# Two attentions in one program: the local scores stored place-minor, the inverses cut in three, two groups of weight splits moved

## The chip, the cores and the metric

The kernel runs on one core of a Trainium2 chip. The metric is the device time of one execution in microseconds (us); three runs of the kernel before gave 1580.18, 1580.74 and 1582.28 us, a median of 1580.74 us.

## The reference

Two independent attention layers over 2048 positions, 32 heads of 18 columns each (576 in all), float32. Layer A is local: each position attends to 8 places, 0, 2, ..., 14 positions back; places before the start are masked. Layer B is full attention without a mask. The two results stand side by side in the output.

```python
# A: W, dil = 8, 2 ; idx = pos - 2 * (0..7)
logits = einsum("bhsd,bhswd->bhsw", q, k[idx]) * scale      # 8 scores per position
attn = softmax(where(idx >= 0, logits, -1e9))
a = einsum("bhsw,bhswd->bhsd", attn, v[idx]) @ wo
# B: full attention
b = einsum(softmax(einsum(q, k) * scale), v) @ wo
out = concatenate([a, b], axis=-1)
```

## The kernel before, in words

**The stages.** First TensorE makes the projections of both layers (to about 416 us). Then come 512 numbered steps, the main part: B's 8 groups of four heads (`NG`), times 4 blocks of 512 queries (`NB`), times 16 tiles of 128 keys (`NT`). The steps end with B's last output product.

**One step.** TensorE makes four scores of 128 keys by 512 queries (L388), the sums of the step before with the values (`weigh`, L898), and two to four score tiles of a later block that serve only to find each query's maximum (L239). ScalarE takes the exponentials of the scores (L398, L401). VectorE (DVE) reduces the tiles of L239 to maxima (L256, L258 and L272): three of them in a plain step. TensorE has few PSUM banks for these tiles, so that it waits when VectorE is behind. Some steps ("producing" ones) also hold products with an output weight (L1239) and take about twice as long.

**Layer A.** The 2048 positions are 8 places `j` of 256 positions (`local(j)`), each held as 128 partitions (32 heads times 4 parts) by 64 positions. Nearly all of it is on GpSimd (POOL): products of queries and shifted keys (`match`, L1042), their sums (L1045), the last sum into the score tile `lg` (L1049, 8 window scores times 64 positions; for j = 0 with masks by L1052), subtraction of the maximum (`lower`, L1065), sums of the exponentials (`total`, L1076), multiplication by the inverse (`share`, L1083), and the weighted values (`weighted`, L1090 to L1096). VectorE finds the maximum over the window in four pieces of 16 positions (`most`, L1059, tile `am`) and the inverses in two pieces of 32 (`inverses`, L1080); ScalarE takes the exponentials (`exponents`, L1069), in two halves in some places and in one piece in others. The result is split into a high and a low part (L1100, L1105) and goes through DRAM to TensorE.

**What sets the order.** Every engine runs its queue in the order in which the program is written. `plan(start, pieces)` puts a piece into the agenda of a step, and `due()` writes the pieces of a step at its end. `local(j)` starts at step 10 + 55 j (`A_FROM`, `GAP`); its pieces have fixed steps within the place: the four maxima at 30 to 33, `lower` at 33, exponentials at 34 and 35, totals at 36, inverses at 37 and 38, `share` at 38, `weighted` from 38 on, the split at 86 and 87 (60 and 61 in the last place). So a piece of GpSimd has no time of its own: GpSimd takes it when all pieces written earlier are done.

**Output weights.** Both `wo` matrices are loaded in five chunks of rows into tile `y` by the DMA queue of SyncE (`load_wo`, L1000) and split three steps later by GpSimd into a high part (a cast, L176) and a low part (a subtraction, L177), into `wohi` and `wolo` for A and into freed tiles `qs` and `ks` for B. A's chunks begin at step 28 and B's at step 404 (`STEPS * (NG - 2) + 20`), one every four steps; the fifth of B has a memset of `y` ahead (L997). The first use of A's splits is the first producing step, of B's the sums of the last group.

Of the kernel before, what the change touches and what calls it, by code (L numbers as in the profile page):

```python
# [7 lines left out]
F32 = mybir.dt.float32  # L8
# [4 lines left out]
AX = mybir.AxisListType  # L13
# [7 lines left out]
W = 8  # L21
DIL = 2
NG = H // 4
# [3 lines left out]
MASKED = -1e9 / SCALE  # L27
# [3 lines left out]
SUB = AB // 4  # L31
HALO = DIL * (W - 1)

STEPS = NB * NT
# [24 lines left out]
def ap(t, *dims):  # L59

    return bass.AP(tensor=t.tensor, offset=t.offset, ap=[list(t.ap[0])] + [list(d) for d in dims])
# [8 lines left out]
def two_attentions(ctx: ExitStack, tc, xa, wa, woa, xb, wb, wob, out):  # L70
# [5 lines left out]
    nc = tc.nc  # L76
# [109 lines left out]
    def plan(start, pieces):  # L186
        for n, f in pieces:
            agenda[start + n].append(f)
# [326 lines left out]
    with (tc.tile_pool(name="x", bufs=1, side="right") as xp,  # L515
# [117 lines left out]
        if True:  # L633

            third = D // 3
# [193 lines left out]
            for k in range(2, 14):  # L829
                n = 46 if k == 2 else 36 + 4 * k  # L830
# [33 lines left out]
            for k, b in order:  # L864
                c = turn_of[k]
                n = min(128, 3 * D - 128 * c)
# [26 lines left out]
    work = ctx.enter_context(tc.tile_pool(name="work", bufs=1, reuse_waits="tile"))  # L893
# [98 lines left out]
    def load_wo(k, src, *pieces):  # L992

        raw = work.tile([128, D], F32, name="y", bufs=4)
        n = 0
        if len(pieces) == 4:
            nc.gpsimd.memset(raw, 0.0)  # L997
            n = 128
        for at, c0, m in pieces:
            load(raw[at : at + m], src[c0 : c0 + m])  # L1000
            n = max(n, at + m)
        if k == "a":
            hi = work.tile([128, D], F32R, name="wohi", bufs=5)
            lo = work.tile([128, D], F32R, name="wolo", bufs=5)
        else:

            c = len(wo.get(k, []))
            hi, lo = (ap(t[:, 0, 0, :] if len(t.shape) == 4 else t[:, 0, :], (1, NB * 1024))[:, D * c : D * c + D]
                      for t in sets[(NG - 3) % 3])
        wo.setdefault(k, []).append((hi, lo))  # L1010
        later(3, lambda: split_on(nc.gpsimd, hi[:n], lo[:n], raw[:n]))


    def local(j):

        st = {}
# [11 lines left out]
        def window(t, c):  # L1028

            return ap(t[:, 2 * c, HALO:], (HALO + SUB, 2), (-DIL, W), (1, SUB))  # L1030

        def wide():
            return work.tile([128, 2, W, SUB], F32, name="pr", bufs=2)

        def match(c):
            if c < DH // 2:
                if c % 2 == 0 and c:
                    room = work.tile([128, DH, SUB], F32, name="aohi", bufs=1)
                    pr = ap(room, (W * SUB, 2), (SUB, W), (1, SUB))
                else:  # L1040
                    pr = wide()
                nc.gpsimd.tensor_mul(pr, ap(st["q"][:, 2 * c], (SUB, 2), (0, W), (1, SUB)), window(st["k"], c))  # L1042
                st["prs"] = st.get("prs", []) + [pr]
            if c > 1:
                nc.gpsimd.tensor_add(st["prs"][0], st["prs"][0], st["prs"][c - 1])  # L1045
            if c == DH // 2:
                st["pr"] = st["prs"][0]
                lg = st["lg"] = work.tile([128, W, SUB], F32, name="lg", bufs=1)
                nc.gpsimd.tensor_add(lg, st["pr"][:, 0], st["pr"][:, 1])  # L1049
                if j == 0:  # L1050
                    for w in range(1, W):
                        nc.gpsimd.memset(lg[:32, w, : DIL * w], MASKED)  # L1052

        def over_window(op, name, i, of):

            if i == 0:
                st[name] = work.tile([128, SUB], F32, name=name, bufs=1)
            at = slice(SUB // of * i, SUB // of * (i + 1))
            nc.vector.tensor_reduce(st[name][:, at], st["lg"][:, :, at].rearrange("p w n -> p n w"), axis=AX.X, op=op)  # L1059

        def most(i, of):
            over_window(ALU.max, "am", i, of)

        def lower():
            nc.gpsimd.tensor_sub(st["lg"], st["lg"], ap(st["am"], (0, W), (1, SUB)))  # L1065

        def exponents(i, of):
            at = slice(W // of * i, W // of * (i + 1))
# [7 lines left out]
            nc.gpsimd.tensor_add(t[:, :half], src[:, :half], src[:, half : 2 * half])  # L1076

        def inverses(n):
            half = st["as"][:, 0, SUB // 2 * n : SUB // 2 * n + SUB // 2]
            nc.vector.reciprocal(half, half)  # L1080

        def share():
            nc.gpsimd.tensor_mul(st["lg"], st["lg"], ap(st["as"], (0, W), (1, SUB)))  # L1083
# [44 lines left out]
        def sums_of_a(h):  # L1128
# [12 lines left out]
            def add():  # L1141
# [7 lines left out]
        MOST = ((30, 0, 4), (31, 1, 4), (32, 2, 4), (33, 3, 4))  # L1149
        EXPS = ((34, 0, 2), (35, 1, 2)) if A_FROM + GAP * j + 35 not in producing else ((35, 0, 1),)  # L1150
        TOTAL = ((36, 0), (36, 1), (36, 2))
        INV = ((37, 0), (38, 1))
        LOWER, SHARE, MATCH, WEIGHT = 33, 38, 5, 38
        UP, REST, PUT0, PUT1 = (60, 61, 64, 66) if j == NJ - 1 else (GAP + 31, GAP + 32, GAP + 34, GAP + 35)
        pieces = [(LOWER, lower), (SHARE, share), (UP, upper), (REST, rest), (PUT0, lambda: put(0)), (PUT1, lambda: put(1))]

        pieces[:0] = [(at, lambda f=f, args=args: f(*args)) for f, ats in ((most, MOST), (exponents, EXPS), (total, TOTAL),
                                                                          (inverses, INV)) for at, *args in ats]
        for c in range(DH // 2 + 1):
            pieces.append((MATCH + 5 * min(c, DH // 2 - 1) // 2, lambda c=c: match(c)))  # L1160
# [8 lines left out]
        for n in range(2):  # L1169
            free, begin = turns[-1] if turns else 0, start + PUT1 + 5  # L1170
            at = max(free, begin)
# [172 lines left out]
        sums[t, b, h] = (y,)  # L1344

    for k, src, start, chunks in (
        ("a", woa, 28, [[(0, 128 * c, 128)] for c in range(4)] + [[(64 * r, 512, 64) for r in range(2)]]),
        ("b", wob, STEPS * (NG - 2) + 20,
         [[(0, 126 * c, 126)] for c in range(4)] + [[(32 * i, 504 + DH * i, DH) for i in range(4)]]),
    ):  # L1350
        plan(start, [(4 * c, lambda k=k, src=src, ch=ch: load_wo(k, src, *ch)) for c, ch in enumerate(chunks)])
    for j in range(NJ):
        plan(A_FROM + GAP * j, local(j))
# [31 lines left out]
    while step < ALL:  # L1385
        n, kt = divmod(step, NT)
        g, b = divmod(n, NB)
# [10 lines left out]
        a = left // 2 if left != 1 or given[0] >= given[1] else 1  # L1398
# [73 lines left out]
```

## Time and profile before

| what | value |
|---|---|
| median of 3 runs | 1580.74 us (1580.18 to 1582.28) |
| the profiled execution's own time | 1580.53 us |
| its span from first to last instruction | 1578.7 us |
| TensorE clock granted in it | 1.000 |
| TensorE, VectorE, ScalarE, GpSimd busy | 99%, 89%, 75%, 61% of the span |
| the 512 steps | from about 416 us to the end |

The rows that the prediction quotes have, in a timeline, the start in us, the length in us, engine, line, operation, the tiles (written from read), the count, and in brackets how long the engine was idle before and who released it. Neighbouring equal instructions are merged into one row. An instruction of VectorE starts before the one ahead has ended, so that from start to start it takes less than its length. In a table of groups the columns are count, busy time in us, mean length in ns, and the idle time before.

### The profile page before, as it was taken

The page shows a single profiled execution, that of the slowest core. Times are in us where ns is not written, and L with a number is a line of the kernel's source. Part 1 is how long each engine was busy: PE and PEld are TensorE (multiplying, and loading weights), DVE is VectorE, ACT ScalarE, POOL GpSimd, SP SyncE. Part 2 cuts the span into 40 slices and gives each one's busy share as a digit, 9 for nine tenths or more (in the row PEclk, how much of TensorE's full clock was granted, in tenths as well). Part 3 has the DMA queues.
Part 4 walks back from the last instruction along what each step waited for, and adds up shares of the span by engine and source line. Part 5 has one row for each costly group of instructions (what it writes and reads, how often), then busy time and mean ns, then how long its engine had stood idle before and what let it go on. Part 6 is the DMA issues. An engine that isn't in the chain of part 4 may idle for free.

```text
span 1578.7 us, 34691 instructions
## 1 busy us (share of the span) xinstructions
PE 1570.7 (99%) x13400; PEld 950.1 (60%) x13400; DVE 1397.6 (89%) x2381; ACT 1183.5 (75%) x1918; POOL 966.0 (61%) x820
## 2 busy tenths in 40 slices
PE   9999999999999999999999999999999999999998
PEld 7999998888544444445444445444444454555776
DVE  5299999999999999999999999999999999999433
ACT  7323441211699999999999999999999999898444
POOL 2305852201257997994996995995995997930100
PEclk9999999999999999999999999999999999999999
DMA  9848954523321253253235316423523142234211
GB/s 263 220 131 208 261 183 126 162 75 100 75 56 55 64 115 90 70 141 100 60 88 145 81 47 155 104 61 103 136 58 98 37 109 71 78 118 157 86 39 61
DMA packets 190149, 173.12 MB, mean 110 GB/s; under 512 B 123120, under 2 KB 136944, under 8 KB 188256
## 3 DMA queue, kind: packets, MB, share of 16 engines
q1 hardware_dynamic: 185120, 159.36, 36.3%
q0 software_dynamic: 4032, 10.63, 3.1%
q8 instruction: 105, 1.72, 0.5%
q10 hardware_dynamic: 832, 0.92, 0.2%
q14 instruction: 60, 0.49, 0.1%
HBM read 97.47 MB, written 72.95 MB: 108 GB/s over the span
## 4 chain that ended last, share of the span: by engine, by line
PE 96%; POOL 2%; DMA 1%; DVE 1%; issue 1%; ACT 0%; SPq 0%; POOLq 0%; ACTq 0%; DVEq 0%
PE po L898 31%; PE bank L239 19%; PE bank L498 16%; PE bank L388 10%; PE bank L1239 8%; PE pair L388 7%; PE bank L424 4%; POOL pr L1045 1%; POOL aohi L1042 0%; DMA first<-xb 0%; DMA raw<-wa 0%; DVE mx L256 0%; POOL ks L177 0%; POOL ohi L844 0%; DMA da<-ohi 0%
## 5 line engine op out<-in xcount | busy, mean ns | idle before, releaser
L239 PE MATMUL bank<-ks,qs 54*128 54x256 f32 (+1 forms) x2526 | 755.1, 372 | 1.3 <-DVE mx L256 0.6
L256 DVE TENSOR_REDUCE mx<-bank 128x1 f32<-128x512 f32 x1024 | 679.9, 684 | 59.5 <-PE bank L239 33.5
L239 PEld LDWEIGHTS bank<-ks,qs 54*128 54x128 f32 x2526 | 414.1, 184 | 428.4 <-DVE mx L272 312.5
L398 ACT ACTIVATE e<-bank 128x512 f32<-128x512 f32 x1024 | 611.2, 603 | 72.9 <-PE bank L388 66.0
L898 PE MATMUL po<-ee,v 128*19 128x512 f32 x2048 | 536.7, 599 | 0.0
L898 PE MATMUL po<-e,v 128*19 128x512 f32 x2048 | 531.4, 599 | 0.0
L401 ACT ACTIVATE ee<-pair 128x1024 f32<-128x1024 f32 x478 | 487.7, 1020 | 1.1 <-PE pair L388 0.4
L388 PE MATMUL bank<-qs,ks 56*128 56x512 f32 x1092 | 460.8, 441 | 0.0
L258 DVE TENSOR_REDUCE mx<-bank 128x2 f32<-128x512 f32 x546 | 355.8, 684 | 20.2 <-PE bank L239 7.2
L272 DVE TENSOR_REDUCE mx<-bank 128x2 f32<-128x512 f32 x478 | 326.1, 682 | 0.0
L388 PE MATMUL pair<-qs,ks 56*128 56x512 f32 x956 | 248.3, 396 | 0.0
L388 PEld LDWEIGHTS bank<-qs,ks 56*128 56x128 f32 x1092 | 194.4, 183 | 15.6 <-ACT e L398 7.1
L1090 POOL TENSOR_TENSOR pr<-lg,akv 128x1024 f32<-128x1024 f32 x72 | 157.2, 2205 | 0.6
L840 ACT ACTIVATE ohi<-bank 128x512 f32<-128x512 f32 (+1 forms) x56 | 30.6, 595 | 147.5 <-issue 125.5
L388 PEld LDWEIGHTS pair<-qs,ks 56*128 56x128 f32 x956 | 137.8, 185 | 0.0
L898 PEld LDWEIGHTS po<-ee,v 128*19 128x19 f32 x2048 | 69.6, 96 | 109.6 <-issue 109.6
L498 PE MATMUL bank<-xhi,ahi 64*128 64x512 f32 x448 | 116.1, 390 | 0.1
L498 PE MATMUL bank<-xlo,ahi 64*128 64x512 f32 (+1 forms) x448 | 104.1, 392 | 0.2 <-POOL xlo L546 0.2
L498 PE MATMUL bank<-xhi,alo 64*128 64x512 f32 x416 | 102.3, 390 | 0.0
L1042 POOL TENSOR_TENSOR pr<-aq,akv 128x1024 f32<-128x1024 f32 x40 | 87.7, 2199 | 17.0 <-PE bank L239 15.9
L1092 POOL TENSOR_TENSOR pr<-pr 128x512 f32<-128x512 f32 x72 | 91.3, 1293 | 0.6
L546 POOL TENSOR_TENSOR alo<-raw,ahi 128x512 fp32r<-128x512 f32 x13 | 16.8, 1294 | 113.1 <-ACT ahi L545 111.8
(210 smaller groups left out, 2369.5 us busy)
## 6 DMA issues: line engine op xcount, KB each, us to landing
do<-n SPq DMA_DIRECT2D x28, 512.0 KB
da<-ohi SPq DMA_DIRECT2D x52, 256.0 KB
akv<-da SPq DMA_DIRECT2D x64, 175.5 KB
out<-y SPq DMA_DIRECT2D x32, 288.0 KB
qs<-dqk SPq DMA_DIRECT2D x30, 288.0 KB
ks<-dqk SPq DMA_DIRECT2D x30, 288.0 KB
at<-dao SPq DMA_DIRECT2D x64, 128.0 KB
rec<-drec SPq DMA_DIRECT2D x29, 256.0 KB
```

The lines of the kernel that those rows point to most:

```text
L239: return nc.tensor.matmul(ps, qs[rows_, b, p, 128 * t : 128 * t + 128], ks[rows_, p, 512 * k + at : 512 * k + at + n], start=True, stop=True)
L256: nc.vector.tensor_reduce(mx[:, r, p, t, k : k + 1], ps, axis=AX.X, op=ALU.max)
L258: nc.vector.tensor_reduce(mx[:, r, p, t, 2 * k - 2 : 2 * k], ps.rearrange("q (h n) -> q h n", h=2), axis=AX.X, op=ALU.max)
L272: nc.vector.tensor_reduce(mx[:, :, p, t, 2 * k - 2 + i], ps.rearrange("q (h n) -> q h n", h=2), axis=AX.X, op=ALU.max)
L388: nc.tensor.matmul(ps, ks[at, p, 128 * kt : 128 * kt + 128], qs[at, b, p], start=True, stop=True)
L398: nc.scalar.activation(e, ps, AF.Exp, scale=SCALE)
L401: nc.scalar.activation(whole, both_scores[0], AF.Exp, scale=SCALE)
L498: nc.tensor.matmul(ps, a, b, start=start, stop=stop)
L898: nc.tensor.matmul(po[32 * i : 32 * i + 19], vs[g][:, kt, 19 * i : 19 * i + 19], es[i], start=kt == 0, stop=kt == NT - 1)
L1090: nc.gpsimd.tensor_mul(at, ap(st["lg"], (0, 2), (SUB, W), (1, SUB)), window(st["v"], n))
L1092: nc.gpsimd.tensor_add(at[:, :, :4], at[:, :, :4], at[:, :, 4:])
L1239: nc.tensor.matmul(sums_[r], a, b, start=i == 0, stop=i == len(both[r]) - 1)
```

## The change

GpSimd's last sum of a place goes into a new tile `lgt` (`by` in the code) in which the 8 window scores of a position stand side by side (64 positions times 8), written with a stride of 32 bytes; the masks of place 0 go there too. `most` reads this tile, so that the 8 values of a maximum are neighbours and not 256 bytes apart. `lower` reads it with a stride of 32 bytes and writes `lg` in the old layout; what follows is as before. The inverses are three pieces of 22, 21 and 21 positions at 37, 38 and 39, and `share` and all of `weighted` move by one step, from 38 to 39. The chunks of A's output weight begin at step 2 (before: 28), those of B's at step 459 (before: 404).

```diff
-                lg = st["lg"] = work.tile([128, W, SUB], F32, name="lg", bufs=1)
-                nc.gpsimd.tensor_add(lg, st["pr"][:, 0], st["pr"][:, 1])
+                st["lg"] = work.tile([128, W, SUB], F32, name="lg", bufs=1)
+                by = st["by"] = work.tile([128, SUB, W], F32, name="lgt", bufs=1)
+                nc.gpsimd.tensor_add(by.rearrange("p n w -> p w n"), st["pr"][:, 0], st["pr"][:, 1])
                 if j == 0:
                     for w in range(1, W):
-                        nc.gpsimd.memset(lg[:32, w, : DIL * w], MASKED)
+                        nc.gpsimd.memset(by[:32, : DIL * w, w], MASKED)
...
-            nc.vector.tensor_reduce(st[name][:, at], st["lg"][:, :, at].rearrange("p w n -> p n w"), axis=AX.X, op=op)
+            nc.vector.tensor_reduce(st[name][:, at], st["by"][:, at], axis=AX.X, op=op)
...
         def lower():
-            nc.gpsimd.tensor_sub(st["lg"], st["lg"], ap(st["am"], (0, W), (1, SUB)))
+            nc.gpsimd.tensor_sub(st["lg"], st["by"].rearrange("p n w -> p w n"), ap(st["am"], (0, W), (1, SUB)))
...
         def inverses(n):
-            half = st["as"][:, 0, SUB // 2 * n : SUB // 2 * n + SUB // 2]
-            nc.vector.reciprocal(half, half)
+            third = st["as"][:, 0, (0, 22, 43)[n] : (22, 43, SUB)[n]]
+            nc.vector.reciprocal(third, third)
...
-        INV = ((37, 0), (38, 1))
-        LOWER, SHARE, MATCH, WEIGHT = 33, 38, 5, 38
+        INV = ((37, 0), (38, 1), (39, 2))
+        LOWER, SHARE, MATCH, WEIGHT = 33, 39, 5, 39
...
-        ("a", woa, 28, [[(0, 128 * c, 128)] for c in range(4)] + [[(64 * r, 512, 64) for r in range(2)]]),
-        ("b", wob, STEPS * (NG - 2) + 20,
+        ("a", woa, 2, [[(0, 128 * c, 128)] for c in range(4)] + [[(64 * r, 512, 64) for r in range(2)]]),
+        ("b", wob, STEPS * (NG - 1) + 11,
```

On GpSimd's queue at the end of the matches of the last place, j = 7, these rows stood before (`y`, `qs` and `ks` are B's output weight and its two parts; `o`, `n` and `rec` belong to B's blocks; the rest is the place's own):

```order
L1042 TENSOR_TENSOR pr<-aq,akv 128x1024
L1045 TENSOR_TENSOR pr<-pr,aohi 128x1024
L936 TENSOR_TENSOR o<-o,rec 128x512
L937 CAST n<-o 128x512
L176 CAST qs_3591<-y 126x576
L177 TENSOR_TENSOR ks_3592<-y,qs_3591 126x576
L997 MEMSET y 128x576
L1042 TENSOR_TENSOR aohi<-aq,akv 128x1024
L1045 TENSOR_TENSOR pr<-pr 128x1024
L1045 TENSOR_TENSOR pr<-pr,aohi 128x1024
L1049 TENSOR_TENSOR lg<-pr 128x512
```

Now the same stretch of GpSimd's queue reads so, with the score tile as its last row:

```order
L1042 TENSOR_TENSOR pr<-aq,akv 128x1024
L1045 TENSOR_TENSOR pr<-pr,aohi 128x1024
L936 TENSOR_TENSOR o<-o,rec 128x512
L937 CAST n<-o 128x512
L1042 TENSOR_TENSOR aohi<-aq,akv 128x1024
L1045 TENSOR_TENSOR pr<-pr 128x1024
L1045 TENSOR_TENSOR pr<-pr,aohi 128x1024
L1050 TENSOR_TENSOR lgt<-pr 128x8x64
```

The split and the memset are gone from here, as are the three splits ahead of them in the same place; all five now stand behind the whole work of the place. A's five splits have gone the other way, to the front of place 0: three ahead of its first match, one behind its second, one behind its third.

On VectorE's queue in place 1 the inverses (tile `as`) stood before so, among the maxima of B (`mx`):

```order
L258 TENSOR_REDUCE mx<-bank_9232 128x2
L1080 RECIPROCAL as<-as 128x32
L258 TENSOR_REDUCE mx<-bank_9248 128x2
L272 TENSOR_REDUCE mx<-bank_9242 128x2
L258 TENSOR_REDUCE mx<-bank_9263 128x2
L1080 RECIPROCAL as<-as 128x32
L256 TENSOR_REDUCE mx<-bank_9285 128x1
L272 TENSOR_REDUCE mx<-bank_9278 128x2
L256 TENSOR_REDUCE mx<-bank_9300 128x1
L933 RECIPROCAL den<-den 128x16
L282 TENSOR_REDUCE m_82<-mx 128x16
```

Now the same stretch of VectorE's queue reads:

```order
L258 TENSOR_REDUCE mx<-bank_9235 128x2
L1081 RECIPROCAL as<-as 128x22
L258 TENSOR_REDUCE mx<-bank_9251 128x2
L272 TENSOR_REDUCE mx<-bank_9245 128x2
L258 TENSOR_REDUCE mx<-bank_9266 128x2
L1081 RECIPROCAL as<-as 128x21
L256 TENSOR_REDUCE mx<-bank_9281 128x1
L272 TENSOR_REDUCE mx<-bank_9274 128x2
L256 TENSOR_REDUCE mx<-bank_9296 128x1
L1081 RECIPROCAL as<-as 128x21
L933 RECIPROCAL den<-den 128x16
```

The third piece stands one step behind the second, and GpSimd's `share`, which needs all pieces, with it. The order of TensorE's and ScalarE's instructions is the same in both kernels.

## Prediction

> **What bounds the kernel now.** I read the page's head, its busy times and the chain of work that ended last, first.
>
> ```profile
> span 1578.7 us, 34691 instructions
> PE 1570.7 (99%) x13400; PEld 950.1 (60%) x13400; DVE 1397.6 (89%) x2381; ACT 1183.5 (75%) x1918; POOL 966.0 (61%) x820
> PE 96%; POOL 2%; DMA 1%; DVE 1%; issue 1%; ACT 0%; SPq 0%; POOLq 0%; ACTq 0%; DVEq 0%
> ```
>
> The chain is TensorE nearly throughout. None of the edits touches a TensorE instruction, so they can only shorten or lengthen steps in which TensorE is held up by another engine. I looked for such steps in VectorE's timeline, at the small maxima `am` of place 2.
>
> ```profile
> 722.13 0.68 DVE L272 TENSOR_REDUCE mx<-bank 128x2 f32<-128x512 f32 x1
> 722.73 1.49 DVE L256 TENSOR_REDUCE mx<-bank 128x1 f32<-128x512 f32 x2
> 724.14 0.68 DVE L272 TENSOR_REDUCE mx<-bank 128x2 f32<-128x512 f32 x1
> 724.74 0.68 DVE L256 TENSOR_REDUCE mx<-bank 128x1 f32<-128x512 f32 x1
> 725.34 0.37 DVE L1059 TENSOR_REDUCE am<-lg 128x16 f32<-128x128 f32 x1
> 725.62 0.68 DVE L256 TENSOR_REDUCE mx<-bank 128x1 f32<-128x512 f32 x1
> 726.22 0.68 DVE L272 TENSOR_REDUCE mx<-bank 128x2 f32<-128x512 f32 x1
> ...
> 728.30 0.68 DVE L272 TENSOR_REDUCE mx<-bank 128x2 f32<-128x512 f32 x1
> ```
>
> From L272 to L272 is one step. A plain one takes 2.01 us (722.13 to 724.14), and there VectorE has time left: three maxima of 0.60 us from start to start (724.14 to 724.74) make 1.80, so 0.21 us is spare. With an `am` the step takes 2.08 us (724.14 to 726.22, and again to 728.30): an `am` takes 0.29 us from start to start (725.34 to 725.62), 0.08 more than is spare. Here VectorE sets the step, by 0.08 us. That is the size of what this change can win in a place.
>
> **The change part by part.** The prices come from the groups of instructions.
>
> ```profile
> L256 DVE TENSOR_REDUCE mx<-bank 128x1 f32<-128x512 f32 x1024 | 679.9, 684 | 59.5 <-PE bank L239 33.5
> ...
> L1059 DVE TENSOR_REDUCE am<-lg 128x16 f32<-128x128 f32 x32 | 11.9, 373 | 0.5 <-POOL lg L1049 0.5
> ...
> L1049 POOL TENSOR_TENSOR lg<-pr 128x512 f32<-128x512 f32 x8 | 10.3, 1285 | 0.6
> ...
> L282 DVE TENSOR_REDUCE m<-mx 128x16 f32<-128x96 f32 x32 | 7.8, 243 | 0.4
> ...
> L177 POOL TENSOR_TENSOR ks<-y,qs 126x576 fp32r<-126x576 f32 (+1 forms) x5 | 7.1, 1422 | 0.4
> ...
> L933 DVE RECIPROCAL den<-den 128x16 f32<-128x16 f32 x29 | 7.0, 243 | 0.0
> ...
> L1080 DVE RECIPROCAL as<-as 128x32 f32<-128x32 f32 x16 | 5.5, 343 | 0.0
> ...
> L176 POOL CAST qs<-y 126x576 fp32r<-126x576 f32 (+1 forms) x5 | 3.3, 666 | 0.0
> ...
> L737 POOL MEMSET vs<- 128x128 f32 x4 | 1.4, 380 | 17.1 <-DMA dv<-vs 17.1
> ...
> L997 POOL MEMSET y<- 128x576 f32 x1 | 0.6, 588 | 0.0
> ...
> L314 POOL MEMSET m<- 128x32 f32 x2 | 0.2, 114 | 0.0
> ```
>
> *Term A, the small maxima.* L282 also makes 16 outputs, from 96 neighbouring values, in 243 ns; L256 takes 684 for 512. Between them lie 1.06 ns a value, so 128 neighbouring values should take 277 ns, against 373 with the wide stride: 96 ns less. From start to start that is 0.29 - 0.10 = 0.19 us, which fits into the spare 0.21. So the overrun of 0.08 us goes. The first of a place's four is partly taken up by the idle time ahead of it, so I count 26 of 32: 26 x 0.08 = 2.1 us won. The ends: nothing (the stride is not what makes it slow) and 32 x 0.08 = 2.6 us.
>
> [...]
>
> *Term B, the inverses.* L1080 and L933 differ by 16 values and 100 ns, 6.25 ns each, so pieces of 22 and 21 take about 280 ns: 24 x 0.28 = 6.7 us in place of 16 x 0.343 = 5.5. A piece of 32 exceeds the spare time by little and two in succession are mostly absorbed; three shorter ones fit, but the third joins steps that have another small operation (in place 1 `den` and `m`). The ends are 16 x (0.343 - 0.28) = 1.0 us won and 6.7 - 5.5 = 1.2 us lost. I take 0.2 us won, near the middle.
>
> *Term C, B's splits leave place 7.*
>
> ```profile
> 1316.38 0.68 DVE L272 TENSOR_REDUCE mx<-bank 128x2 f32<-128x512 f32 x1
> ...
> 1318.14 0.39 DVE L1059 TENSOR_REDUCE am<-lg 128x16 f32<-128x128 f32 x1 [0.49 <-POOL lg L1049]
> ...
> 1319.05 0.68 DVE L272 TENSOR_REDUCE mx<-bank 128x2 f32<-128x512 f32 x1
> ```
>
> This is the only place where VectorE waits for GpSimd's score tile, 0.49 us, and the step takes 2.67 us (1316.38 to 1319.05), 0.66 over a plain one. Four splits and the memset leave the queue ahead of that tile: 4 x (0.67 + 1.42) + 0.59 = 8.9 us earlier, far more than is needed. Won: 0.66 us; at least 0.49. Their new place is behind the place's work, where GpSimd is free and the sums that need them are more than ten steps off. SyncE's queue is passed too: the chunk loads stand among the loads of the last group, and the latest of these, `rec`, moves back by the four short loads of the fifth chunk; what GpSimd makes of `rec` waits for TensorE afterwards anyway. Cost nothing; without that cover some 2 us.
>
> *A's splits* go where GpSimd waits now:
>
> ```profile
> 427.94 4.35 POOL L1042 TENSOR_TENSOR pr<-aq,akv 128x1024 f32<-128x1024 f32 x2 [15.87 <-PE bank L239]
> ...
> 452.16 0.21 POOL L176 CAST mt<-mt 128x32 fp32r<-128x32 f32 x1 [19.87 <-DVE mt L290]
> ```
>
> Of 36 us idle the first four splits take 8.4 and the three chunk loads ahead of the matches delay these a little; the `mt` at 452 comes no later. The fifth split takes the room of one that stood among place 0's matches before, so the tile of place 0 is ready as early as now. Nothing won, nothing lost.
>
> *Term D, `share` one step later.*
>
> ```profile
> 490.54 1.27 POOL L1049 TENSOR_TENSOR lg<-pr 128x512 f32<-128x512 f32 x1
> ...
> 496.13 0.38 DVE L1059 TENSOR_REDUCE am<-lg 128x16 f32<-128x128 f32 x1
> ...
> 513.41 1.28 POOL L1083 TENSOR_TENSOR lg<-lg,as 128x512 f32<-128x512 f32 x1 [2.58 <-DVE as L1080]
> ...
> 605.39 1.30 POOL L1049 TENSOR_TENSOR lg<-pr 128x512 f32<-128x512 f32 x1
> ...
> 607.72 0.38 DVE L1059 TENSOR_REDUCE am<-lg 128x16 f32<-128x128 f32 x1
> ```
>
> Between the third and the fourth of these rows the view by stretches of time gives the busy time of TensorE, its weight loads, VectorE, ScalarE and GpSimd, in this order:
>
> ```profile
> 513.41:606.69 93.28, 93.28 (x737) 41.09 (x740) 88.17 (x147) 92.33 (x139) 91.90 (x69) 1.00 0.40 92
> ```
>
> From place 0's `share` to the score tile of place 1 GpSimd is busy 91.90 of 93.28 us. It has nothing to catch up with: what moves `share` moves the tile. The third piece comes one step, 2.0 us, after the second and is 0.07 shorter, so `share` is 1.93 us later against the steps. The tile ended at 606.69, 1.03 us ahead of its `am`: now the `am` comes first and VectorE waits 1.93 - 1.03 = 0.9 us. Behind it stand B's maxima, and TensorE waits for those; the spare 0.2 us of the step is taken off: **0.7 us lost**, in place 1 alone. In the other places the tile is ready 4 us or more ahead, as in place 0 (491.81 against 496.13); place 7 gains by term C. The ends: nothing (GpSimd catches up after all) and 0.9.
>
> *Terms E and F, GpSimd's strides of 32 bytes.* No row shows such a sum. The nearest is the memset L737, whose values lie 76 bytes apart: 380 ns for 128, where L997 and L314 (588 for 576, 114 for 32, so 0.87 ns each) would give 198. That is 1.4 ns a value more, 0.73 us for 512 values. Or nothing, as a sum at 1285 ns takes 2.5 ns a value already and the write may hide below it. I take 0.35 us for each, the middle, since a sum moves three streams of which one changes. For the score tile (E) it adds to the wait of place 1: 0.35 us lost. For `lower` (F) ScalarE is next:
>
> ```profile
> 502.95 1.28 POOL L1065 TENSOR_TENSOR lg<-lg,am 128x512 f32<-128x512 f32 x1 [4.26 <-DVE am L1059]
> ...
> 504.37 0.43 ACT L1069 ACTIVATE lg<-lg 128x256 f32<-128x256 f32 x1
> ...
> 614.62 1.27 POOL L1065 TENSOR_TENSOR lg<-lg,am 128x512 f32<-128x512 f32 x1 [4.09 <-DVE am L1059]
> ...
> 616.04 0.43 ACT L1069 ACTIVATE lg<-lg 128x256 f32<-128x256 f32 x1
> ...
> 1207.20 1.28 POOL L1065 TENSOR_TENSOR lg<-lg,am 128x512 f32<-128x512 f32 x1 [1.83 <-DVE am L1059]
> ...
> 1208.62 0.43 ACT L1069 ACTIVATE lg<-lg 128x256 f32<-128x256 f32 x1
> ```
>
> In places 0, 1 and 6 the first exponential starts 0.14 us after `lower` ends (504.37 against 504.23); the `am` ahead is 0.10 shorter, so 0.24 us is free. Longer by 0.35, `lower` holds ScalarE, and B's exponentials behind it, 0.1 us in each of the three: 0.3 us lost. The ends for E and F together: nothing, and 0.73 + 3 x 0.49 = 2.2.
>
> [...]
>
> *The sum.* Won 2.1 + 0.2 + 0.66 = 2.96; lost 0.7 + 0.35 + 0.3 = 1.35; together 1.6 us won. The profiled execution took 1580.53 us by itself, so 1578.9; the median of the runs stands 0.2 us above it. I predict **1579.1 us**.
>
> **The rivals.** *First, GpSimd does not hold place 1 back*: strides cost nothing and the wait of term D is absorbed by idle time that the sums hide. Then 2.96 us are won, 1580.74 - 2.96 = 1577.8 us, and with term A at its end and B's 1.0 as far as 1576.5. For it: place 1's next steps hold a copy that waits for TensorE in any case. Against it: GpSimd's 91.90 busy us of 93.28.
>
> *Second, the other side: GpSimd's strided sum is slow.* If each of the two takes L us longer, the loss is L in place 1 and L - 0.24 in three places: 0.7 + L + 3 (L - 0.24). It meets the 2.96 won at L = 0.75, just above the bound from L737. At twice the time of now, L = 1.28, it is 0.7 + 1.28 + 3.1 = 5.1, net 2.1 us lost: 1582.9 us; at L = 1.6 it is over 0.2%. For it: the one strided row takes nearly twice the time. Against it: 1285 ns leaves room to hide it. [...]
>
> *Third, `am` does not get shorter.* Then A is 0 and the sum is 0.5 us lost: 1581.2 us. L282 reads few values, too, and may not stand for it.
>
> **How the numbers follow.** I give my forecast (within 1 us of 1579.1) 0.50, the first rival 0.25, the second 0.15, the third 0.10. A measurement of this kernel tells about 0.2%, 3.2 us, from no change: below 1577.6 or above 1583.9 us. Of the first rival half, 0.13, ends below 1577.6, and I add 0.07 for a larger term A or B under my forecast: faster 0.20. Of the second, half, 0.08, ends above 1583.9, and I add 0.02 for a wait that I have not seen: slower 0.10. The rest, 0.70, is no change. The range, 1576.9 to 1581.8 us, leaves out the first rival's far end and most of the second.
>
> **What the profile after would show.** A: L1059 at about 277 ns, steps around it of 2.01 us. B: 24 inverses of about 280 ns. C: no idle time ahead of place 7's first `am`. D: VectorE idle about 0.9 to 1.3 us ahead of place 1's first `am`, released by GpSimd's tile. E, F: the tile and `lower` at 1.3 to 2.0 us, idle time of ScalarE ahead of the first exponential of places 0, 1 and 6. A row of `am` at 370 ns would take A away; a tile over 2 us would make the kernel slower.

## The result, and the profile after

The changed kernel takes **1578.18 us** (median, 1577.69 to 1578.78), the kernel before, beside it, 1580.93 us: a ratio of 0.9981 with a 95% interval of 0.9974 to 0.9989 (over all runs, so not quite that of the two medians). That is 2.75 us less; 1.6 had been forecast. The profiled executions took 1577.96 and 1580.53 us, 2.57 us apart. The head of the page after:

```profile
span 1576.2 us, 34697 instructions
PE 1568.2 (99%) x13400; PEld 947.9 (60%) x13400; DVE 1394.8 (88%) x2389; ACT 1183.3 (75%) x1918; POOL 968.8 (61%) x820
PE 92%; DMA 3%; POOL 2%; issue 1%; DVE 1%; SPq 1%; ACT 0%; POOLq 0%; ACTq 0%; DVEq 0%
```

TensorE is still the chain. The groups with the changed operations (count, busy us, mean ns, idle time before them):

```profile
L1060 DVE TENSOR_REDUCE am<-lgt 128x16 f32<-128x128 f32 x32 | 8.8, 275 | 0.7 <-POOL lgt L1050 0.7
L1081 DVE RECIPROCAL as<-as 128x21 f32<-128x21 f32 x16 | 4.4, 277 | 0.0
L1081 DVE RECIPROCAL as<-as 128x22 f32<-128x22 f32 x8 | 2.2, 279 | 0.0
...
L1066 POOL TENSOR_TENSOR lg<-lgt,am 128x512 f32<-128x512 f32 x8 | 12.5, 1560 | 45.8 <-DVE am L1060 45.8
L1050 POOL TENSOR_TENSOR lgt<-pr 128x512 f32<-128x512 f32 x8 | 10.4, 1297 | 0.6
```

An `am` takes 275 ns (before 373), the inverses 277 to 279, the tile 1297 (before 1285), `lower` 1560 (before 1281). VectorE at place 2, where a step with an `am` took 2.08 us before:

```profile
724.44 0.68 DVE L272 TENSOR_REDUCE mx<-bank 128x2 f32<-128x512 f32 x1
725.04 0.68 DVE L256 TENSOR_REDUCE mx<-bank 128x1 f32<-128x512 f32 x1
725.64 0.28 DVE L1060 TENSOR_REDUCE am<-lgt 128x16 f32<-128x128 f32 x1
725.83 0.69 DVE L256 TENSOR_REDUCE mx<-bank 128x1 f32<-128x512 f32 x1
726.44 0.68 DVE L272 TENSOR_REDUCE mx<-bank 128x2 f32<-128x512 f32 x1
```

From L272 to L272 it is 2.00 us, and the `am` takes 0.19 us from start to start (725.64 to 725.83). VectorE at the first `am` of places 1 and 7:

```profile
608.20 0.28 DVE L1060 TENSOR_REDUCE am<-lgt 128x16 f32<-128x128 f32 x1 [0.70 <-POOL lgt L1050]
...
1316.20 0.27 DVE L1060 TENSOR_REDUCE am<-lgt 128x16 f32<-128x128 f32 x1
```

The wait has left place 7 and stands in place 1, 0.70 us long.

To see where the time went, every step's length was worked out from TensorE's timeline: step k runs from the start of the k-th group of eight L898 products to the next, counted from 0 at about 416 us. Up to step 0 the executions differ by up to 1.1 us (416.3 to 417.4; 1.0 between two profiles of the changed kernel itself), so the last column starts there. By the program's numbers steps 44, 99 and 374 have the first exponential of places 0, 1 and 6, steps 95 and 96 the first two `am` of place 1 and step 425 the first of place 7; what step 80 waits for is told at e9. All in us:

| kernel | steps 44, 99, 374 | step 80 | 95 + 96 | step 425 | step 0 to the end |
|---|---|---|---|---|---|
| before | 2.03, 2.04, 2.03 | 2.17 | 4.38 | 2.67 | 1162.43 |
| after | 2.20, 2.19, 2.19 | 2.18 | 4.78 | 2.01 | 1159.84 |
| e1 layout only | 2.19, 2.20, 2.20 | 2.17 | 4.28 | 2.58 | 1160.58 |
| e2 splits only | 2.04, 2.05, 2.03 | 2.18 | 4.38 | 2.08 | 1161.37 |
| e3 inverses only | 2.02, 2.03, 2.02 | 2.66 | 4.57 | 4.54 | 1165.10 |
| e4 after, two pieces | 2.20, 2.19, 2.18 | 2.18 | 4.28 | 2.00 | 1159.41 |
| e5 `lower` in halves | 2.20, 2.18, 2.19 | 2.83 | 4.28 | 1.99 | 1159.90 |
| e6 `am` of four | 2.19, 2.18, 2.19 | 2.17 | 4.26 | 2.53 | 1160.49 |
| e7 `share` at 40 | 2.19, 2.20, 2.18 | 2.18 | 4.72 | 2.00 | 1159.52 |
| e8 strides by place | 2.19, 2.19, 2.18 | 2.59 | 4.45 | 2.01 | 1160.90 |
| e9 third inverse at 40 | 2.19, 2.19, 2.18 | 3.86 | 4.28 | 2.01 | 1164.56 |
| e10 A's splits only | 2.03, 2.05, 2.02 | 2.19 | 4.39 | 2.59 | 1162.01 |
| e11 pairs, two pieces | 2.19, 2.18, 2.18 | 2.18 | 4.28 | 2.01 | 1159.31 |
| e12 after again | 2.18, 2.19, 2.19 | 2.53 | 4.48 | 2.00 | 1159.96 |

### The profile page after: what moved, and what is told of

It reads as the page before. It is cut to its first block, busy times and chain, and to the rows that moved or that the text cites. A ratio compares the mean times of both kernels' runs of the same rounds, so it can differ in the third digit from the quotient of the medians.

```text
span 1576.2 us, 34697 instructions
## 1 busy us (share of the span) xinstructions
PE 1568.2 (99%) x13400; PEld 947.9 (60%) x13400; DVE 1394.8 (88%) x2389; ACT 1183.3 (75%) x1918; POOL 968.8 (61%) x820
## 4 chain that ended last, share of the span: by engine, by line
PE 92%; DMA 3%; POOL 2%; issue 1%; DVE 1%; SPq 1%; ACT 0%; POOLq 0%; ACTq 0%; DVEq 0%
PE po L898 30%; PE bank L239 19%; PE bank L498 15%; PE bank L388 9%; PE bank L1240 8%; PE pair L388 7%; PE bank L424 4%; DMA drec<-den 1%; DMA ks<-dqk 1%; POOL pr L1045 1%; POOL xlo L546 1%; DMA raw<-xa 0%; DMA rec<-drec 0%; DVE mx L256 0%; PE bank L664 0%
## 5 line engine op out<-in xcount | busy, mean ns | idle before, releaser
L256 DVE TENSOR_REDUCE mx<-bank 128x1 f32<-128x512 f32 x1024 | 679.5, 683 | 59.7 <-PE bank L239 33.2
L898 PE MATMUL po<-ee,v 128*19 128x512 f32 x2048 | 536.7, 599 | 0.0
L898 PE MATMUL po<-e,v 128*19 128x512 f32 x2048 | 531.4, 599 | 0.1
L401 ACT ACTIVATE ee<-pair 128x1024 f32<-128x1024 f32 x478 | 487.6, 1020 | 0.5
L272 DVE TENSOR_REDUCE mx<-bank 128x2 f32<-128x512 f32 x478 | 325.6, 681 | 0.0
L898 PEld LDWEIGHTS po<-ee,v 128*19 128x19 f32 x2048 | 69.6, 96 | 110.0 <-issue 110.0
L652 POOL TENSOR_TENSOR olo<-olo,ohi 128x512 fp32r<-128x512 f32 x36 | 46.2, 1295 | 65.5 <-ACT ohi L651 52.8
```

Of the source, the lines that this page charges most:

```text
L256: nc.vector.tensor_reduce(mx[:, r, p, t, k : k + 1], ps, axis=AX.X, op=ALU.max)
L272: nc.vector.tensor_reduce(mx[:, :, p, t, 2 * k - 2 + i], ps.rearrange("q (h n) -> q h n", h=2), axis=AX.X, op=ALU.max)
L401: nc.scalar.activation(whole, both_scores[0], AF.Exp, scale=SCALE)
L898: nc.tensor.matmul(po[32 * i : 32 * i + 19], vs[g][:, kt, 19 * i : 19 * i + 19], es[i], start=kt == 0, stop=kt == NT - 1)
```

## The experiments

**e1, the layout alone.** The kernel before with the four hunks on `lgt`, `am` and `lower`.

> The kernel before with only the score tile laid out side by side (`lgt`, the `am` that read it, `lower` that reads it); inverses in two pieces, `share` at step 38, splits where they were. Theory 1 (the prediction's terms, with the sizes read in the two traces): the 32 `am` at about 280 ns win 2.1 us in their steps, `lower` at about 1.55 us costs about 0.16 us in places 0, 1 and 6 (0.5 us together), place 1's tile is about 1 us ahead of its `am`, and place 7 still waits about 0.4 us: 1.6 us under the kernel before, some 1579.3 us. Rival (the loss in place 1 comes from the strided tile and not from the later `share`): step 95 or 96 is 0.3 to 0.4 us longer here too, with VectorE idle ahead of place 1's first `am`, and the gain is 1.2 us.

Measured: 1579.40 us against 1581.07 (ratio 0.9988, 0.9979 to 0.9996), 1.85 us less from step 0. Place 1 has no wait (95 + 96 take 4.28 us, less than before), so the loss there is not from the strided tile. Place 7 still waits. Steps 44, 99 and 374 are 0.16 longer here already.

**e2, the splits alone.**

```diff
-        ("a", woa, 28,
+        ("a", woa, 2,
...
-        ("b", wob, STEPS * (NG - 2) + 20,
+        ("b", wob, STEPS * (NG - 1) + 11,
```

> The kernel before with only the splits of the two output weights moved. Theory 1: place 7's tile ends some 6 us ahead of its `am`, its first step goes from 2.67 to 2.01 us, and nothing else changes by more than 0.1 us: 0.67 us under the kernel before. Rival (the chunk loads that now stand among the last group's loads, and A's splits ahead of place 0's matches, hold something back): a gain of 0.66 in place 7 and a loss of 0.3 to 2 us at the end or in place 0, so no gain or a loss.

Measured: 1579.82 us against 1581.07 (0.9989, 0.9980 to 0.9998), 1.06 less from step 0. Step 425 gives 0.60. The rest was not expected: steps 239, 356 and 443 are about 0.2 us shorter each and step 326 0.2 longer (e10).

**e3, the inverses alone.**

```diff
-        INV = ((37, 0), (38, 1))
-        LOWER, SHARE, MATCH, WEIGHT = 33, 38, 5, 38
+        INV = ((37, 0), (38, 1), (39, 2))
+        LOWER, SHARE, MATCH, WEIGHT = 33, 39, 5, 39
```

> The kernel before with only the inverses in three pieces, and `share` and the weighted sums one step later. Theory 1: `share` and all that follows on GpSimd is about 1.7 us later against the steps, so place 1's first `am` waits about 0.5 us and its step is 0.4 us longer; place 7, which waited 0.49 us already, waits about 1.5 us longer if GpSimd has no idle time between, so step 425 grows by 1 to 1.7 us; the inverses' steps win about 0.3 us. Together 1.1 to 1.8 us over the kernel before. Rival (GpSimd catches up before place 7 and only place 1 is hit): about 0.1 us over. Second rival (the third piece costs more than the two longer ones did): a further 0.5 us or more in the steps of the inverses.

Measured: 1585.07 us against 1581.07 (1.0020, 1.0011 to 1.0028), 2.67 more from step 0 in the profiled execution (4.0 by the medians), which is more than expected. Most of it, 1.87 us, is place 7, whose `am` waited 0.49 us before:

```profile
1318.18 0.68 DVE L256 TENSOR_REDUCE mx<-bank 128x1 f32<-128x512 f32 x1
1321.25 0.37 DVE L1059 TENSOR_REDUCE am<-lg 128x16 f32<-128x128 f32 x1 [2.39 <-POOL lg L1049]
```

It now waits 2.39: GpSimd's delay of one step reaches place 7 in full and step 425 is 1.87 us longer. The inverses' own steps win nothing: 0.08 in step 48 and in step 432, against 0.15 lost in step 104, where the third piece of place 1 stands beside `den`. And step 80 is longer by 0.5 us, which no theory had; e9 comes back to it.

**e4, the changed kernel with two inverses.** The edit of e3 taken back.

> The changed kernel with the inverses back in two pieces and `share` back at step 38, so the layout and the moved splits without the third edit. Theory 1: against the changed kernel the loss of 0.4 us in place 1 goes and the 0.3 us of shorter inverses is given back, 0.14 us of it in place 1 not: 0.1 to 0.3 us under the changed kernel, about 2.8 us under the kernel before. Rival (three pieces are worth more than they cost): 0.3 us or more over the changed kernel. If the three edits add up, this run minus the kernel before is the sum of the layout's and the splits' runs.

Measured: 1577.74 us against 1581.07 (0.9980, 0.9971 to 0.9990), 0.43 us under the changed kernel from step 0: 0.49 in steps 95 and 96, while the short pieces' gains in steps 48 and 432 and their loss in step 104 (0.12 each way) cancel; the rest are differences below 0.06 us in a step. The layout and the splits add up: 1.85 + 1.06 = 2.91 against 3.02 here. The inverses do not: alone they cost 2.67 us, beside the other two 0.43, since the moved splits take the wait out of place 7.

**e5, `lower` in two halves.** The table's steps 44, 99 and 374 are those of the first exponential in places 0, 1 and 6. Term F said that `lower` holds ScalarE there. This kernel lets `lower` end earlier.

```diff
-        def lower():
-            nc.gpsimd.tensor_sub(st["lg"], st["by"].rearrange("p n w -> p w n"), ap(st["am"], (0, W), (1, SUB)))
+        def lower(i):
+            at = slice(SUB // 2 * i, SUB // 2 * (i + 1))
+            nc.gpsimd.tensor_sub(st["lg"][:, :, at], st["by"][:, at].rearrange("p n w -> p w n"),
+                                 ap(st["am"][:, at], (0, W), (1, SUB // 2)))
...
-        pieces = [(LOWER, lower), ...
+        pieces = [(LOWER - 1, lambda: lower(0)), (LOWER, lambda: lower(1)), ...
```

> The changed kernel with `lower` in two halves of 32 columns, the first a step earlier, so that it ends some 0.7 us earlier against the steps. The steps of the first exponential of places 0, 1 and 6 (steps 44, 99 and 374) went from 2.04 us before to 2.20 after. Theory F1 (the prediction's term F: ScalarE waits for the slower `lower`): these three steps go back to about 2.04 us and the kernel is 0.5 us under the changed one. Theory F2 (ScalarE itself is full: with the exponential it needs 2.19 us of a step, and before the change the steps of 2.08 us ahead of it, which the longer `am` set, had let it get ahead): the three steps stay at 2.20 us and nothing is won.

Measured: 1578.70 us against 1581.09 (0.9990, 0.9981 to 0.9999). GpSimd's second half takes 0.7 us less than the whole did:

```profile
L1067 POOL TENSOR_TENSOR lg<-lgt,am 128x256 f32<-128x256 f32 x16 | 14.1, 879 | 37.0 <-DVE am L1060 36.9
```

In place 0 it ends at 503.97 us, and the first exponential starts at 504.71, 0.74 us later, so ScalarE does not wait for it. The three steps stay at 2.20, 2.18 and 2.19 us. F1 falls, F2 stands.

**e6, `am` of four scores.**

```diff
-            ... st["lg"][:, :, at].rearrange("p w n -> p n w"), axis=AX.X, op=op)
+            ... st["lg"][:, : W // 2, at].rearrange("p w n -> p n w"), axis=AX.X, op=op)
```

> The kernel before, with the old layout, inverses and splits; only `am` is taken over the first four of the eight local scores instead of all eight (the true maximum of the rest is left out), so that an `am` gets shorter while `lower` keeps its 1.28 us. Theory F2 (ScalarE has no room left once the steps of `am` are 2.01 us): steps 44, 99 and 374 grow from 2.04 to 2.20 us although `lower` is as fast as before; with an `am` of 0.20 us from start to start the sum is 2.1 won less 0.5 lost, 1.6 us under the kernel before, as with the layout alone. Theory F1 (the slower `lower` holds ScalarE): these three steps stay at 2.04 us and 2.1 us are won. If an `am` of half the values at the wide stride still takes over 0.21 us from start to start, both are a little smaller.

Measured: 1579.11 us against 1581.09 (0.9984, 0.9975 to 0.9993), 1.94 less from step 0.

```profile
L1065 POOL TENSOR_TENSOR lg<-lg,am 128x512 f32<-128x512 f32 x8 | 10.2, 1280 | 41.0 <-DVE am L1059 41.0
...
L1059 DVE TENSOR_REDUCE am<-lg 128x16 f32<-128x64 f32 x32 | 8.3, 258 | 0.5 <-POOL lg L1049 0.5
```

`lower` is as fast as before, and the three steps still grow to 2.19, 2.18 and 2.19 us. So the loss comes with the shorter `am`, whatever `lower` takes. ScalarE's timeline of the changed kernel at step 44 shows what fills it:

```profile
502.71 1.02 ACT L401 ACTIVATE ee<-pair 128x1024 f32<-128x1024 f32 x1
503.62 0.61 ACT L398 ACTIVATE e<-bank 128x512 f32<-128x512 f32 x1
504.10 0.43 ACT L1070 ACTIVATE lg<-lg 128x256 f32<-128x256 f32 x1
504.40 0.61 ACT L398 ACTIVATE e<-bank 128x512 f32<-128x512 f32 x1
504.88 1.05 ACT L401 ACTIVATE ee<-pair 128x1024 f32<-128x1024 f32 x1
```

From one L401 to the next it is 2.17 us (502.71 to 504.88) without a gap: 0.30 for A's exponential and 1.87 for B's three. In a plain step of 2.00 us only 0.13 is spare. The kernel before needs the same stretch of 2.16 us (502.99 to 505.15):

```profile
502.99 1.02 ACT L401 ACTIVATE ee<-pair 128x1024 f32<-128x1024 f32 x1
...
505.15 1.05 ACT L401 ACTIVATE ee<-pair 128x1024 f32<-128x1024 f32 x1
```

But there step 43, the last of the four steps of `am`, starts at 503.05 us and takes 2.09, and ScalarE enters it 0.06 us early. In the changed kernel step 43 takes 2.00 us, and ScalarE enters it at its start. These 0.09 and 0.07 us are the 0.16 that step 44 now takes longer: the long steps of `am` had covered them. This is read from the two traces; that `lower` is not the cause is shown by the runs.

**e7, `share` at step 40.**

```diff
-        LOWER, SHARE, MATCH, WEIGHT = 33, 39, 5, 39
+        LOWER, SHARE, MATCH, WEIGHT = 33, 40, 5, 40
```

> The changed kernel with `share` and the weighted sums at step 40 in place of 39, that is one step of 2.0 us later again with nothing added. Theory D (GpSimd has nothing to catch up with between place 0's `share` and place 1's tile, whose lead is 0.03 us now): the idle time of VectorE ahead of place 1's first `am` grows from 0.70 us to 2.7 us, step 95 from 2.36 to 4.4 us, and the kernel is 2.0 us over the changed one; the other places have 3.2 us or more to spare and stay as they are. Rival (GpSimd catches up in part): under 1 us over the changed one.

Measured: 1578.32 us against 1581.09 (0.9982, 0.9973 to 0.9990), as the changed kernel. Theory D's 2.0 us did not come, and the rival's number holds for another reason than its own: there was no delay to catch up with. Third inverse and `share` of place 0 in this kernel:

```profile
514.97 0.28 DVE L1081 RECIPROCAL as<-as 128x21 f32<-128x21 f32 x1
...
515.40 1.28 POOL L1084 TENSOR_TENSOR lg<-lg,as 128x512 f32<-128x512 f32 x1 [6.53 <-DVE as L1081]
```

GpSimd stands idle 6.53 us and starts `share` when the third inverse ends, as in the changed kernel. The step number of a GpSimd piece only gives its place in the queue. What made `share` later in this change is the third inverse at step 39 of VectorE, not its own number.

**e8, strides by place.** In place j a tile in blocks of B positions, so that a position's scores stand 4 B bytes apart.

```diff
+        B = (1, 1, 2, 4, 8, 16, 1, 1)[j]
...
+        def blocks(t):
+            return ap(t, (B, W), (W * B, SUB // B), (1, B))
...
+            if j == 6:
+                nc.gpsimd.tensor_sub(st["lg"].rearrange("p w n -> p n w"), st["by"], ap(st["am"], (1, SUB), (0, W)))
```

> The changed kernel with a layout of its own for the score tile in places 2 to 6, to price strides: in place 2 the eight scores of a position stand 8 bytes apart, in place 3 16, in place 4 32, in place 5 64 bytes (with runs of 2, 4, 8 and 16 neighbouring values for GpSimd); in place 6 `lower` goes in the order of the side-by-side tile, so that it reads neighbours and writes 256 bytes apart. Known: `am` takes 277 ns at 4 bytes and 373 at 256, `lower` 1.28 us with both streams in order and 1.55 with a read 32 bytes apart. [...] Rival (only wide strides cost): 277 up to 64 bytes. `lower`: if the distance from value to value is what costs, runs of 2 give about 1.4 us and runs of 8 or 16 about 1.3; in place 6 the write costs nothing (as the tile's did) and `lower` takes 1.3 us.

Measured: 1579.29 us in a single run, which is here for the prices of single operations alone. The second `am` of places 2 to 6 (strides of 8, 16, 32, 64 and 4 bytes), then `lower` of places 0 and 2 to 6:

```profile
728.05 0.28 DVE L1073 TENSOR_REDUCE am<-lgt 128x16 f32<-128x128 f32 x1
844.93 0.37 DVE L1073 TENSOR_REDUCE am<-lgt 128x16 f32<-128x128 f32 x1
964.27 0.38 DVE L1073 TENSOR_REDUCE am<-lgt 128x16 f32<-128x128 f32 x1
1083.32 0.37 DVE L1073 TENSOR_REDUCE am<-lgt 128x16 f32<-128x128 f32 x1
1202.51 0.28 DVE L1071 TENSOR_REDUCE am<-lgt 128x16 f32<-128x128 f32 x1
```

```profile
502.85 1.54 POOL L1083 TENSOR_TENSOR lg<-lgt,am 128x512 f32<-128x512 f32 x1 [7.58 <-DVE am L1071]
732.50 1.30 POOL L1085 TENSOR_TENSOR lg<-lgt,am 128x512 f32<-128x512 f32 x1 [7.72 <-DVE am L1073]
850.31 1.28 POOL L1085 TENSOR_TENSOR lg<-lgt,am 128x512 f32<-128x512 f32 x1 [6.82 <-DVE am L1073]
968.95 1.28 POOL L1085 TENSOR_TENSOR lg<-lgt,am 128x512 f32<-128x512 f32 x1 [7.30 <-DVE am L1073]
1087.91 1.27 POOL L1085 TENSOR_TENSOR lg<-lgt,am 128x512 f32<-128x512 f32 x1 [7.50 <-DVE am L1073]
1206.87 1.14 POOL L1081 TENSOR_TENSOR lg<-lgt,am 128x512 f32<-128x512 f32 x1 [1.57 <-DVE am L1071]
```

VectorE's price is a step between 8 bytes (0.28 us) and 16 (0.37), and flat from there to 64 (0.37 to 0.38). The rival, which had 277 ns up to 64 bytes, is refuted; what makes the step is not shown. GpSimd's `lower` takes 1.54 us with a lone value 32 bytes from the next, against 1.28 in order, and 1.30 with runs of two, where 1.4 had been expected. In place 6, reading neighbours, with each maximum repeated eight times in a row, and writing 256 bytes apart, `lower` takes 1.14 us, less than with both streams in order and than the 1.3 expected.

**e9, the third inverse at step 40.**

```diff
-        INV = ((37, 0), (38, 1), (39, 2))
-        LOWER, SHARE, MATCH, WEIGHT = 33, 39, 5, 39
+        INV = ((37, 0), (38, 1), (40, 2))
+        LOWER, SHARE, MATCH, WEIGHT = 33, 40, 5, 40
```

> The changed kernel with the third inverse, `share` and the weighted sums at step 40 in place of 39. `share` at 40 alone moved nothing, so what sets its time is the third inverse on VectorE, not its own step number. Theory D: with the third inverse a step of 2.0 us later, `share` of place 0 and with it the tile of place 1 come 2.0 us later, VectorE's idle time ahead of place 1's first `am` grows from 0.70 to about 2.7 us, and the kernel is 2.0 us over the changed one. Rival (GpSimd catches up): under 1 us over it.

Measured: 1581.97 us against 1580.91 (1.0006, 0.9997 to 1.0015); the changed kernel beside it (e12) 1578.88. By the medians that is 3.1 us over the changed kernel, and 4.7 from step 0 in the profiled execution, which is a long one of its ten (1583.48 us; 1579.73 to 1586.34). GpSimd does not catch up, and the loss exceeds the 2.0 us expected. But place 1 shows nothing: its tile is 0.71 us ahead of its `am`. TensorE has lost 3.2 us already, in steps 80 to 82: 1.7 in step 80 and 1.5 in the two behind it. What it waited for there (us in total, times, longest):

```profile
PE bank L239 <- DMA do<-n: 1.3, 1, 1.3
```

The 1.5 us behind the wait fall in a stretch, from 582.8 to 586.1 us, in which TensorE runs at half its clock. The view by stretches of time has the busy time of TensorE, its weight loads, VectorE, ScalarE and GpSimd, then the granted clock, 0.50 here and 1.00 in the changed kernel, and two numbers on DMA:

```profile
582.80:586.10 3.30, 3.30 (x20) 1.51 (x16) 1.63 (x4) 1.47 (x2) 3.22 (x2) 0.50 0.49 110
```

No other of these profiles has such a stretch within the 512 steps. What brings it on is not shown: here step 80 is 1.69 us longer than before, e3's step 425 was 1.87 us longer, and the mean clock of e3's execution was 1.00.

The wait itself comes from SyncE's queue, which waits for GpSimd's high and low parts of a block's maxima (`mt`) before it stores them. That wait in the kernel before and in this one:

```profile
SPq L300 <- POOL mt L177: 7.0, 1, 7.0
```

```profile
SPq L300 <- POOL mt L177: 10.7, 1, 10.7
```

SyncE's timeline, the issue of that store, in the kernel before, the changed kernel and this one:

```profile
550.17 1.17 SPq L300 DMA_DIRECT2D dm<-mt  x2
```

```profile
551.68 1.15 SPq L300 DMA_DIRECT2D dm<-mt  x2
```

```profile
554.47 1.14 SPq L300 DMA_DIRECT2D dm<-mt  x2
```

`mt` stands in GpSimd's queue behind `share` and part of `weighted`; behind SyncE's wait stand ten loads of the next group's `qs` and `ks`, two of `qs` from `dm`, and `do<-n`. The lead of L300 on the start of step 80 is 27.6 to 27.7 us in the seven kernels with two inverses, and step 80 takes 2.17 to 2.19; in the six with three, the last at step 39, it is 25.8, and step 80 takes 2.18 to 2.83; here it is 23.95, and it takes 3.86. So there is a second way from a late GpSimd to TensorE, and its slack is used up by the change to the point where executions differ: 2.18 us in the first profile of the changed kernel, 2.53 in the second (e12), with 95 + 96 shorter by 0.30 in turn, as TensorE is late already. Which of the transfers TensorE waits for is not settled; the view names the one that lands last. In steps 143 and 207 a further 0.97 and 0.96 us go against the changed kernel; 1.0 of this the view of waits puts down to `at<-dao`, A's results on their way back through DRAM.

**e10, A's splits alone.** The first line of e2's edit.

> The kernel before with only the splits of the first output weight moved (start 2 in place of 28). Open is where the 0.4 us come from that both splits together won outside place 7 (steps 239, 356 and 443 shorter by 0.2 us, step 326 longer by 0.2). Theory 1 (the splits of the first weight are worth nothing): these steps stay as before, nothing over 0.1 us changes, and the time is that of before. Rival (they come from the first weight's move): steps 239, 356 and 443 are 0.2 us shorter here too and the kernel is some 0.4 us under the one before.

Measured: 1580.37 us against 1580.91 (1.0000, 0.9991 to 1.0009). Steps 239, 356 and 443 are 0.16 to 0.20 us shorter, 326 is 0.19 longer, and 469 too: the rival is right on where the steps change, and the sum stays below what a measurement tells. What differs is one instruction of ScalarE. At step 356, in the kernel before and in this one:

```profile
1169.54 1.20 ACT L398 ACTIVATE e<-bank 128x512 f32<-128x512 f32 x2
1170.84 1.02 ACT L401 ACTIVATE ee<-pair 128x1024 f32<-128x1024 f32 x1
```

```profile
1169.56 1.20 ACT L398 ACTIVATE e<-bank 128x512 f32<-128x512 f32 x2
1170.66 1.02 ACT L401 ACTIVATE ee<-pair 128x1024 f32<-128x1024 f32 x1
```

L401 starts 0.10 us after the end of the row ahead (1170.74) in the one and 0.10 before it (1170.76) in the other. Nothing that the profile shows releases it. It is the same steps in every kernel with A's splits moved and in none without; the cause stays open.

**e11, pairs and two pieces.** Runs of two positions are cheap for both engines in e8, so this kernel has them in every place, with e4's inverses.

```diff
+        def pairs(t):
+            return ap(t, (2, W), (2 * W, SUB // 2), (1, 2))
...
+            nc.gpsimd.tensor_sub(plain(st["lg"]), pairs(st["by"]), ap(st["am"], (0, W), (2, SUB // 2), (1, 2)))
```

> The changed kernel with the inverses back in two pieces, and the score tile laid out in pairs of positions, so that a position's eight scores stand 8 bytes apart: in the run of strides that gave an `am` of 0.28 us and a `lower` of 1.28 us, the best of both layouts. Theory F2 (ScalarE is full in the steps of the exponentials): the faster `lower` is worth nothing, steps 44, 99 and 374 stay at 2.20 us, and the time is that of the run with two pieces, 0.4 us under the changed kernel. Theory F1 (`lower` holds ScalarE): these steps come back to 2.04 us and it is 0.9 us under the changed kernel.

Measured: 1577.72 us against 1580.91 (0.9981, 0.9972 to 0.9990).

```profile
L1073 POOL TENSOR_TENSOR lg<-lgt,am 128x512 f32<-128x512 f32 x8 | 10.4, 1299 | 53.6 <-DVE am L1066 53.6
...
L1066 DVE TENSOR_REDUCE am<-lgt 128x16 f32<-128x128 f32 x32 | 8.8, 276 | 0.0
```

Both operations are at their low price, and the time is e4's: steps 44, 99 and 374 stay at 2.19, 2.18 and 2.18. F2 again.

**e12, the changed kernel beside e11.**

> The changed kernel itself, on the same chip as the run in pairs with two pieces, so that these two are compared directly: as measured, about 2.7 us under the kernel before, and 0.4 us over the run in pairs.

Measured: 1578.88 us against 1580.91 (0.9991, 0.9983 to 1.0000). That is 2.0 us under the kernel before, where 2.7 had been expected. e11 is 1.16 us under it by the medians and 0.65 from step 0, 0.54 of it in steps 80, 95 and 96, but the intervals overlap: that two pieces beat three is shown by the steps, not by the times.

## Why the prediction was right, and where its steps were not

The time came out 0.9 us under the forecast, within its range, and 0.17% under the kernel before. By the steps of the prediction, in us from the step lengths of the two first profiles:

| term | forecast | measured |
|---|---|---|
| A, small maxima | -2.1 | -2.05 in 24 steps |
| B, inverses | -0.2 | 0.0 (e3: 48 and 432 against 104) |
| C, place 7 | -0.66 | -0.67 |
| A's splits | 0 | -0.57 in steps 239, 267, 326, 356, 443 (most of them in e10 too; why is open) |
| D, place 1 | +0.7 | +0.40 in steps 95 and 96 |
| E, strided tile | +0.35 | 0 |
| F, `lower` | +0.3 | +0.48, but from ScalarE |
| the rest | | -0.2 |
| sum | -1.6 | -2.6 |

That the total came so near owes something to luck. The 0.57 us of A's splits have no mechanism in the prediction, and the 0.48 lost at the first exponentials was near in size but has another cause. The misses of D, E and A's splits all lie on one side, 1.2 us together. The time alone stands nearer to the first rival's 1577.8 us than to the forecast. What speaks against that rival is place 1, where VectorE does wait 0.70 us and 0.40 us are lost, which it had at nothing.

**A** was right in price, mechanism and nearly in count: 277 ns forecast, 275 measured, 24 shorter steps in place of 26, and e6 wins the same steps with another way of making `am` short. The slope behind the 277 runs from a row that reads SBUF (L282) to one that reads a PSUM bank (L256), so that it came out so close may be luck. **B** failed as a choice between its ends: the third piece in a step with `den` takes back what the shorter pieces give. **C** was exact.

**D** was right in mechanism and too large. `share` came 1.66 us later in time, 1.9 against the steps, as forecast; the stretch from `share` to place 1's tile was 0.18 shorter (91.80 against 91.98), so the wait was 0.70 and not 0.9. Of that the step's spare 0.2 and the `am`'s own 0.10 go off. What D missed is the second way, over SyncE and the loads of step 80. It takes its part ahead of place 1 in some executions, and the two overlap instead of adding up.

**E** failed: 32 bytes between written values cost GpSimd 12 ns in 1285. The memset of `vs`, from which the bound came, does not stand for a sum. The first rival was right on this point.

**F** failed in its mechanism, though its size was near. `lower` does take 0.28 us longer, but ScalarE does not wait for it (e5, e6, e11): the steps of the first exponentials take 2.18 to 2.20 us once the steps ahead of them are plain ones, and in step 44 ScalarE works for 2.17 us without a gap. The prediction asked what a longer `lower` holds up and not what a shorter VectorE uncovers. Reading one stream of two at 32 bytes from value to value costs `lower` a good fifth (1.28 to 1.56 us), and nothing of it reaches the time.

The second rival, a slow strided sum, was far from its point: L is 0.01 us for the tile and 0.28 for `lower`, where 0.75 was needed. The third, an `am` that does not get shorter, is refuted by L1060.

## What to carry to other kernels

Where one engine sets a step by a few hundredths, ask which engine is next: half a microsecond of the 2.1 won on VectorE went to ScalarE, which had only 0.13 us to spare in a plain step. A late GpSimd reached TensorE by two ways here, the score tile (VectorE waits 0.70 us for it at place 1 in the changed kernel) and SyncE's loads (in e9 the lead of L300 fell from 27.6 to 23.95 us and step 80 took 3.86 us against 2.17), so its slack was the smaller of the two and not that of the tile in view. Price edits together: the third inverse costs 2.7 us alone and 0.4 beside the moved splits.

## What the runs showed of the hardware

- VectorE's maximum over 8 values from SBUF took 0.27 to 0.29 us for 128 values at 4 or 8 bytes apart (the changed kernel, e11) and 0.36 to 0.40 at 16, 32, 64 and 256 (e8, the kernel before).
- GpSimd's sum with 512 outputs took 1.297 us writing 32 bytes apart, against 1.285 in order. Its subtraction with 512 outputs took 1.56 us reading one stream 32 bytes apart, against 1.28 in order, and 1.30 with runs of two values.
- A subtraction on GpSimd whose second operand repeats one value 8 times in a row and whose output goes 256 bytes apart took 1.14 us, against 1.28 with all in order.
- At step 356 ScalarE started an exponential of 128x1024 0.10 us after the end of the row ahead in the kernel before and 0.10 us before it with A's splits moved (e10), with nothing in the profile that releases it.
- TensorE's granted clock was 0.50 for some 3.3 us behind a wait of 1.3 us in one execution (e9); in another, whose step 425 was 1.87 us longer than before (e3), its mean was 1.00.
